# Fixed instruction lists for the first ten attention steps and the first MLP group

## The chip, the cores and the metric

One core of a Trainium2 chip runs the whole program. The metric is device time in microseconds (us), the median of several executions. One execution is also recorded by the hardware profiler, and every row below is read from that recording.

TensorE (PE; its weight loads are listed as PEld), VectorE (DVE), ScalarE (ACT), GpSimd (POOL) and SyncE (SP, which here only issues DMAs) each work off their own instruction stream in order, and wait on semaphores for one another.

## What is computed

Sliding-window attention with sinks, and then an MLP on its output:

```python
scores = q @ k.T / sqrt(64)                     # 4 batches, 8 heads, 768 tokens, 64 wide
keep   = (key < n_sink) | (0 <= query - key < window)     # n_sink 4, window 128
a      = softmax(where(keep, scores, -1e9))
x      = (a @ v) rearranged to [3072 tokens, 512]
h      = x @ w_in                               # 512 -> 2048
g      = h * erf(softplus(h))
out    = g @ w_out                              # 2048 -> 512
```

q, k and v arrive as float32. w_in and w_out arrive as float64, so every weight has to be rebuilt as float32 from the two 32-bit words of the double, by integer operations on VectorE.

## The kernel before

**Tiling.** The 3072 tokens are cut into 12 groups of 256 (three for each batch). Attention works on a group and a pair of heads at a time: a **step** s is group s // 4, pair s % 4, so there are 48. The MLP works on a group at a time, in 16 **blocks** of 128 hidden columns.

**A step** goes through these functions. `load` (L184) issues the DMAs of q, k and v: four for q and k, two for v, and two more for the sink rows of v in the first group of a batch. `prep` (L213) transposes q and k on TensorE; ScalarE copies the result to `kq` (L223). In the first group of a batch it also fills `sv` (L228 on ScalarE, L229 on VectorE). `score` (L239) makes the scores with 16 matmuls (L272). Its VectorE part is copy_predicated (L284) and one masked minimum for each of four blocks (L289); ScalarE takes exp (L293); a DMA moves a part of `kq` on for the next group. `norm` (L299) adds 1e-9 to the sum (L302), takes the reciprocal (L303) and scales four blocks (L307), all on VectorE. `ptrans` (L309) transposes the probabilities on TensorE (L317), ScalarE copies them to `pt` (L319), GpSimd cuts `uo` out of them (L323), VectorE makes the split sink part `sh` (L331, L332), which TensorE transposes (L338). `av` (L342) multiplies by v (L353, L361). `xfin` (L365) copies the result to `x` (L372, or L377 and L378).

**The weights.** They are cut into 32 pieces of 128 x 512 (16 of each matrix). `wload` (L421) fetches one piece of 512 KB, `wconv` (L430) makes float32 of it with three VectorE operations (L439, L442, L448), and `wsplit` (L457) makes a high part by a ScalarE cast (L461) and a low part by a VectorE subtract (L462). Raw pieces, float32 pieces and split pieces all take slots of one pool of 33 slots, 4 KB of each partition (`wpool`, tag `wo`). The last four pieces are converted in a work tile and copied over by ScalarE (L455).

**The MLP.** `hidden` (L524) makes one block of h, `act` (L537) the activation of two blocks at a time: six ScalarE passes (L545 to L550) and three VectorE operations (L552). `project` (L561) adds a block's share to the two output tiles. The first group uses the unsplit float32 weights (L529, L570) and needs no split pieces; later groups use the split ones (L533), and their `act` adds a cast (L557) and a GpSimd subtract (L558).

**The order of the work.** The code hands the whole program to a planner, which draws up each engine's instruction stream by simulated time: of the instructions that are ready it takes the one with the best priority. `at` (L380) sets that from a place `a` on a common scale (256 units for each block) and an offset by kind of work (L45). The first group's 16 blocks have the places 16 to 31, the second group's 32 to 47. `pos` (L385) gives a step's place, the table `plan` (L389) those of its parts. In `make_mlp` an act comes after its two blocks, a projection four blocks (`LAG`) behind its block. The conversions follow a rate (`W0`, L505), with five loads ahead (`WQ`); the splits have fixed places (L419), from 21 to 37 on that scale. Nothing but data ties the order of VectorE, TensorE and SP; only the score and av matmuls of a step are held in one order by `follow` (L204).

Of the kernel before, what the change touches and what calls it, by code (L numbers as in the profile page):

```python
# [19 lines left out]
P = 128  # L20
# [16 lines left out]
W0, W1 = 10, 7  # L37
WQ = 5

# [6 lines left out]
UB = 3  # L46
RING = 2
# [3 lines left out]
def kernel(  # L51
# [38 lines left out]
    for i, s in enumerate((n_sink, window)):  # L90
        nc.scalar.dma_start(words[:, i, :], s.bitcast(I32).partition_broadcast(P))
# [33 lines left out]

    def dcopy(dst, src):
        nc.sync.dma_start(dst, src)

    def fast_path():
        with ExitStack() as st:  # L130
# [51 lines left out]
            stp = {}  # L182

            def load(s):  # L184
                g, c = divmod(s, NPAIR)
                b, gb = divmod(g, GPB)
                d = stp[s] = {}
                for nm, src in (("q", q), ("k", k), ("v", v)):
# [3 lines left out]
                    for h in range(2):  # L192
                        nc.sync.dma_start(
# [3 lines left out]
                if gb == 0:  # L197

                    sr = d["sv"] = d["v"][: 2 * SW, 0].rearrange("p h d -> p (h d)")
                    nc.gpsimd.memset(sr, 0.0)  # L200
                    for h in range(2):
                        nc.sync.dma_start(sr[SW * h : SW * h + SW, 64 * h : 64 * h + 64], v[b, 2 * c + h, :SW, :])
# [10 lines left out]
            def prep(s):  # L213
# [4 lines left out]
                for j, t in enumerate((d["k"], d["q"])):  # L218
                    for i in range(2):
                        nc.tensor.transpose(  # L220
# [3 lines left out]
                if g % GPB == 0:  # L224
                    x = tp[:, 0, :SW].rearrange("p (o t) -> p o t", o=1)
                    nc.scalar.copy(kq[:, c, :3, P:], x.broadcast_to([P, 3, SW]))
                    for r0 in (0, 32):
                        nc.scalar.copy(sv[r0 : r0 + 32, c, :], d["sv"])  # L228
                    nc.vector.tensor_tensor(sv[64:96, c, :], d["sv"], sv[:32, c, :].bitcast(F32), op=ALU.subtract)  # L229

            def core(s):

                prev = None
                if s - AL >= NE:
                    prev = av(s - AL)
                if s < NSTEP:
                    score(s, prev)

            def score(s, prev):  # L239
# [3 lines left out]
                d = stp[s]  # L243
                d["sum"], d["neg"] = (
# [3 lines left out]
                ps, both = [], None  # L248
# [12 lines left out]
                dx = KB + 80  # L261
                X = [80, 80 + dx]
                lo, hi = slice(0, 64), slice(64, P)
                for i in range(2):
                    qt = kq[:, c, 3 + i, :]
                    kt = kq[:, c].rearrange("p n t -> p (n t)")
                    for hf, r0, n, x in ((lo, KB * i, KB + 64, X[i]), (hi, KB * i + 64, KB + 80, X[i] - 80)):
                        for h in (1, 0):
# [3 lines left out]
                                nc.tensor.matmul(ps[h][hf, x : x + n], qt[r, hf], kt[r, r0 : r0 + n], start=True, stop=True),  # L272
                            )

# [451 lines left out]
```

## Time and profile before

| | us |
|---|---|
| median of 3 executions (lowest, highest) | 765.98 (763.82, 767.38) |
| the profiled execution | 765.26 |
| its span, from the first to the last instruction | 763.3 |
| TensorE busy | 718.0 (94%) |
| VectorE busy | 526.5 (69%) |
| ScalarE busy | 535.0 (70%) |
| GpSimd busy | 202.6 (27%) |

The shares are means over the whole span, which has two very different parts: about 130 us in which the weights are fetched and rebuilt and the first group is computed, and the eleven groups after it. A share has to be read for each of the two. A matmul row's length is modelled by the profiler, and consecutive instructions of one engine overlap by about 0.1 us in the rows, so a sum of lengths is a little more than the time taken.

### The profile page before, as it was taken

Reading aid. Unit: us, or ns where it says so; the run is one execution under the profiler, and the core shown is the slowest. Engines: PE = TensorE matmul, PEld = TensorE weight load, DVE = VectorE, ACT = ScalarE, POOL = GpSimd, SP = SyncE. Lnnn points to the kernel's source line nnn. Section 1 sums busy time; section 2 is a strip of 40 time slices with the busy share of each in tenths; the row PEclk is TensorE's granted clock in tenths of the full one; section 3 lists DMA queues with packets and bytes.
Section 4 is the critical chain, followed back from the end, with each engine's and each line's share of the span. In section 5 each row is a group of like instructions: output and inputs, shape, how many; then the busy total and the mean of one; then the engine's idle time right before and its main releaser. Section 6 shows DMA issues by size and latency. Waiting matters only on the chain.

```text
span 763.3 us, 14942 instructions
## 1 busy us (share of the span) xinstructions
PE 718.0 (94%) x5168; PEld 598.2 (78%) x5168; DVE 526.5 (69%) x1509; ACT 535.0 (70%) x1261; POOL 202.6 (27%) x212
## 2 busy tenths in 40 slices
PE   2577998999999999999999999999999999999997
PEld 2345664887888898888888888888888888888885
DVE  6978998888676576576586586586576586584352
ACT  2356578897786687677787687687686687686473
POOL 1211220133322223232322232332322232322122
PEclk8679998999999999999999999999999999999999
DMA  6776530211211211211121211111111111100000
GB/s 203 218 231 198 218 86 15 76 23 26 61 44 31 67 45 25 63 31 32 56 49 30 59 42 37 55 41 29 56 38 42 56 46 36 39 12 1 28 1 32
DMA packets 100595, 47.33 MB, mean 62 GB/s; under 512 B 89248, under 2 KB 93344, under 8 KB 100512
## 3 DMA queue, kind: packets, MB, share of 16 engines
q1 hardware_dynamic: 100224, 46.29, 21.8%
q8 instruction: 43, 0.70, 0.4%
q14 instruction: 40, 0.33, 0.1%
q10 hardware_dynamic: 288, 0.00, 0.0%
HBM read 37.88 MB, written 6.29 MB: 58 GB/s over the span
## 4 chain that ended last, share of the span: by engine, by line
PE 76%; DVE 10%; ACT 6%; DMA 4%; issue 2%; SPq 1%; POOL 1%; ACTq 0%; DVEq 0%; POOLq 0%
PE o L570 30%; PE h L533 27%; PE av L361 5%; PE ps L272 4%; PE tqk L220 3%; PE tp L317 3%; PE h L529 2%; DVE pst L307 2%; DVE acc L552 1%; ACT u L550 1%; DMA ws<-in_moe_w_out_dram 1%; PE ts L338 1%; DVE w L442 1%; ACT pst L293 1%; DMA out_dram<-ot 1%
## 5 line engine op out<-in xcount | busy, mean ns | idle before, releaser
L570 PE MATMUL o<-wt,g 128*128 128x512 f32 x1056 | 270.0, 399 | 1.1 <-POOL g L558 0.5
L570 PEld LDWEIGHTS o<-wt,g 128*128 128x128 f32 x1056 | 189.0, 188 | 36.5 <-POOL g L558 1.3
L533 PE MATMUL h<-xh,wt 128*128 128x256 f32 x1408 | 203.7, 282 | 1.8 <-DVE acc L552 1.1
L533 PEld LDWEIGHTS h<-xh,wt 128*128 128x128 f32 x1408 | 184.7, 189 | 11.4 <-DVE acc L552 1.8
L558 POOL TENSOR_TENSOR g<-acc,g 128x512 fp32r<-128x512 f32 x88 | 114.7, 1303 | 291.7 <-DVE g L557 182.7
L550 ACT ACTIVATE u<-r 128x512 f32<-128x512 f32 x288 | 165.0, 623 | 13.5 <-DVE wf L448 4.4
L323 POOL TENSOR_SCALAR_AFFINE_SELECT uo<-pt 128x512 f32<-128x512 f32 (+1 forms) x96 | 83.1, 887 | 252.5 <-ACT pt L319 231.8
L552 DVE SCALAR_TENSOR_TENSOR acc<-u,acc 128x512 f32<-128x512 f32 x176 | 128.4, 730 | 19.1 <-ACT u L550 2.8
L552 DVE SCALAR_TENSOR_TENSOR acc<-u,h 128x512 f32<-128x512 f32 x88 | 60.4, 687 | 108.3 <-POOL g L558 60.3
L533 PE MATMUL h<-xl,wt 128*128 128x256 f32 x704 | 111.2, 279 | 0.0
L293 ACT ACTIVATE pst<-pst,kq 128x144 f32<-128x144 f32 x192 | 77.4, 405 | 25.7 <-DVE kq L289 24.6
L533 PEld LDWEIGHTS h<-xl,wt 128*128 128x128 f32 x704 | 94.2, 188 | 0.0
L545 ACT ACTIVATE r<-h 128x512 f32<-128x512 f32 x96 | 57.0, 593 | 25.8 <-PE h L533 24.9
L546 ACT ACTIVATE r<-r 128x512 f32<-128x512 f32 x96 | 61.1, 637 | 2.0
L547 ACT ACTIVATE r<-r 128x512 f32<-128x512 f32 x96 | 60.6, 631 | 2.6
L307 DVE TENSOR_SCALAR pst<-pst,kq 128x144 f32<-128x144 f32 x192 | 57.2, 360 | 1.5
L317 PE MATMUL tp<-ident,pst 128*128 128x128 f32 x192 | 36.4, 291 | 17.5 <-DVE pst L307 17.2
L557 DVE CAST g<-acc 128x512 fp32r<-128x512 f32 x88 | 44.3, 504 | 12.1 <-PE o L570 8.1
L223 ACT COPY kq<-tqk 128x512 f32<-128x512 f32 x48 | 28.0, 585 | 33.7 <-PE tqk L220 31.6
L361 PE MATMUL av<-uo,v 128*64 128x128 f32 (+1 forms) x512 | 50.1, 328 | 1.2 <-POOL uo L323 1.2
L377 ACT CAST xh<-av 128x256 fp32r<-128x256 f32 x44 | 16.0, 365 | 49.2 <-PE av L361 49.2
L272 PE MATMUL ps<-kq 64*64 64x208 f32 (+1 forms) x768 | 49.5, 369 | 0.0
(78 smaller groups left out, 723.0 us busy)
## 6 DMA issues: line engine op xcount, KB each, us to landing
ws<-in_moe_w_in_dram SPq DMA_DIRECT2D x16, 512.0 KB, 5.8
ws<-in_moe_w_out_dram SPq DMA_DIRECT2D x16, 512.0 KB, 5.0
q<-in_q_dram SPq DMA_DIRECT2D x96, 64.0 KB, 2.2
k<-in_k_dram SPq DMA_DIRECT2D x96, 64.0 KB, 2.2
v<-in_v_dram SPq DMA_DIRECT2D x64, 96.0 KB, 2.4
out_dram<-ot SPq DMA_DIRECT2D x24, 256.0 KB, 2.0
v<-in_v_dram SPq DMA_DIRECT2D x32, 64.0 KB, 2.2
kq<-kq SPq DMA_DIRECT2D x32, 64.0 KB, 2.0
```

Of the source, the lines that this page charges most:

```text
L272: nc.tensor.matmul(ps[h][hf, x : x + n], qt[r, hf], kt[r, r0 : r0 + n], start=True, stop=True),
L293: nc.scalar.activation(y, y, AF.Exp, bias=d["neg"][:, i, h : h + 1], scale=-1.0, accum_out=d["sum"][:, i, h : h + 1])
L307: nc.vector.tensor_scalar_mul(p, p, sm[:, i, h : h + 1])
L323: nc.gpsimd.affine_select(out=uo[:, :, i1:, e, :], in_=pt[:, :, i1:, :], pattern=[[0, 2], [0, 2 - i1], [-sg, P]], compare_op=op, fill=0.0, ...
L361: prev, nc.tensor.matmul(o, x[:, h, :], y[:, h, :], start=False, stop=(m == len(ops) - 1), skip_group_check=True)
L533: nc.tensor.matmul(o, wt[NC * j + c][:, p, fs], xt[e][:, c, :], start=(m == 0), stop=(m == len(ops) - 1))
L546: nc.scalar.activation(r, r, AF.Square, bias=b_v, scale=-0.5)
L547: nc.scalar.activation(r, r, AF.Square, bias=b_r)
L550: nc.scalar.activation(u, r, AF.Square, bias=b_a[i], scale=CS)
L552: nc.vector.scalar_tensor_tensor(out=acc, in0=u, scalar=CC[i] * CS**2, in1=x, op0=ALU.add, op1=ALU.mult)
L558: nc.gpsimd.tensor_tensor(gl, acc, gh.bitcast(F32), op=ALU.subtract)
L570: nc.tensor.matmul(self.acc[g, i], gt[e][:, n0 : n0 + P], w, start=(f == 0 and m == 0), stop=(f == NF - 1 and m == len(ops) - 1),)
```

## The change

Three lists name the work of the first ten steps and the first group's 16 blocks, one each for SP (`LOADS`), VectorE (`VEC`) and TensorE (`TEN`). In them q and v load a step's q and k, and its v; L loads, C converts a weight piece, D finishes all conversions under way; p, s, t, u and a are prep, score, the two transposes of ptrans and av on TensorE; f, n, w, k, x are the score's VectorE part, norm, `sh`, `sv` and xfin; H, A and P are hidden, act and project. A class `Line` ties each instruction of an engine to the one before it, so the order of the lists is the engine's order. On TensorE that holds to the end of the lists, on SP to place 20, on VectorE to place 50 (`CEND`), which is two blocks into the third group.

Conversions are cut into their three operations, and `fill` puts one operation of each conversion under way between the dependent operations of norm and act. A converted piece is written at once to half of a slot that two pieces share, for all 32. The splits have new places: 26 (cast) and 27.5 (subtract) for the first four, 30 and 31.5 for the next five, then on to 45 and 46.5. Steps 2 and 3 keep their probabilities in pool slots of their own, and the first steps' transposes use other PSUM tiles. Four things change engine: half of the q and k loads of steps 0 and 1 (SP to ScalarE), the two `sv` copies of steps 0 to 3 (ScalarE to GpSimd), and the scaling in norm of steps 4 to 7 (VectorE to ScalarE). Later steps' places move by fractions of a block.

```diff
+CEND = 50.0
 WQ = 5
+HI = 6.0
+LO = 4.5
+LOADS = (
+    "q0 q1 L0 v0 q2 v1 L1 q3 v2 L2 q4 v3 L3 L4 q5 v4 L5 v5 L6 L7 q6 v6 L8 L9 L10 L11 q7 v7 L12 L13 L14 L15 L16 L17 q8 v8 "
+    "L18 L19 L20 L21 L22 q9 v9 L23 L24 L25 L26 L27 L28 L29 L30 L31"
+)
+VEC = (
+    "f0 C0 D f1 n0 w0 n1 w1 k0 f2 k1 C1 D n2 w2 k2 f3 C2 D n3 w3 k3 f4 C3 n4 D f5 w4 C4 C5 n5 D C6 C7 D w5 C8 C9 A1 C10 C11 "
+    "D f6 x4 C12 A3 n6 C13 D w6 C14 C15 A5 C16 C17 D f7 x5 C18 C20 A7 n7 C19 C21 D w7 C22 C23 A9 C24 C25 D f8 x6 C26 A11 n8 "
+    "C27 D w8 C28 C29 A13 x7 C30 C31 D f9 A15"
+)
+TEN = (
+    "p0 s0 p1 s1 p2 t0 u0 s2 t1 u1 p3 a0 x0 s3 a1 x1 t2 u2 p4 s4 a2 x2 t3 u3 p5 s5 a3 x3 t4 u4 H0 H1 H2 H3 p6 t5 u5 a4 s6 "
+    "H4 H5 P0 P1 H6 P2 t6 u6 H7 P3 p7 a5 s7 H8 H9 P4 P5 H10 P6 t7 u7 p8 H11 P7 a6 s8 H12 H13 P8 a7 P9 t8 H14 P10 u8 p9 H15 "
+    "P11 s9"
+)
@@ load @@
-                        nc.sync.dma_start(
+                        (nc.scalar if s < 2 and h and nm != "v" else syn).dma_start(
@@ the lists' order @@
+            class Line:
...
+                    def run(*a, **k):
+                        ins = f(*a, **k)
+                        if self.on:
+                            self.last = follow(self.last, ins)
+                        return ins
...
+            vec, ten, syn = (Line(x) for x in (nc.vector, nc.tensor, nc.sync))
@@ prep, now prep and sinks @@
-                        nc.scalar.copy(sv[r0 : r0 + 32, c, :], d["sv"])
+                        (nc.gpsimd.tensor_copy if s < NE else nc.scalar.copy)(sv[r0 : r0 + 32, c, :], d["sv"])
@@ score @@
+                if s in (2, 3):
+                    t = wpool.tile([P, 2 * DM], F32, tag="wo", name=f"pst_{s}")
...
-                    if s == 1:
+                    if s in (1, 2):
                         ps.append(ps_h.tile([P, 2, GT], F32, tag="h", name=nm).rearrange("p a t -> p (a t)"))
-                    elif s == 2:
-                        ps.append(ps_o.tile([P, DM], F32, tag="o", name=nm))
@@ norm @@
-                nc.vector.tensor_scalar_add(sm, sm, 1.0e-9)
-                nc.vector.reciprocal(sm, sm)
+                vec.tensor_scalar_add(sm, sm, 1.0e-9)
+                fill()
+                vec.reciprocal(sm, sm)
+                fill()
...
+                        if 4 <= s < 8:
+                            nc.scalar.activation(p, p, AF.Copy, scale=sm[:, i, h : h + 1])
+                        else:
+                            vec.tensor_scalar_mul(p, p, sm[:, i, h : h + 1])
@@ ptrans and strans @@
-                tp = ps_t.tile([P, 2, 2, P], F32, tag="t", name=f"tp_{s}")
+                pool, tag = (ps_o, "o") if s < 6 else (ps_t, "t")
+                tp = pool.tile([P, 2, 2, P], F32, tag=tag, name=f"tp_{s}")
@@ wconv @@
+                if wn // 2 not in pair:
+                    pair[wn // 2] = wpool.tile([P, 2, DM], F32, tag="wo", name=f"wf_{wn // 2}")
+                t = wf[n] = pair[wn // 2][:, wn % 2, :]
...
+                vec.tensor_scalar(ti, w[:, :, 1], 0x07FFFFFF, 3, op0=ALU.bitwise_and, op1=ALU.logical_shift_left)
+                yield
+                vec.scalar_tensor_tensor(
+                    out=ti, in0=w[:, :, 1], scalar=-0x40000000, in1=ti, op0=ALU.bitwise_and, op1=ALU.bitwise_or
+                )
+                yield
+                vec.scalar_tensor_tensor(
+                    out=ti, in0=w[:, :, 0], scalar=29, in1=ti, op0=ALU.logical_shift_right, op1=ALU.bitwise_or
+                )
-                wf[n] = wpool.tile([P, 2 * DM], F32, tag="wo", name=f"wf_{n}")[:, :DM]
-                nc.scalar.copy(wf[n], t)
+            def fill():
+                for w in list(todo):
+                    try:
+                        next(w)
+                    except StopIteration:
+                        todo.remove(w)
@@ the places, and the loop over all work @@
+            for n in order:
+                add(LEAD + NF + use(n) - HI, "h", n)
+                add(LEAD + NF + use(n) - LO, "l", n)
+            for a, _, nm, j in sorted(ev):
+                vec.on, ten.on, syn.on = a < CEND, a <= last, a < LEAD + 4
+                what, fn = acts[nm]
+                with at(a, what):
+                    fn(j)
@@ act @@
-                nc.vector.scalar_tensor_tensor(out=acc, in0=u, scalar=CC[i] * CS**2, in1=x, op0=ALU.add, op1=ALU.mult)
+                self.vec.scalar_tensor_tensor(out=acc, in0=u, scalar=CC[i] * CS**2, in1=x, op0=ALU.add, op1=ALU.mult)
+                self.fill()
```

## Rows read from the trace of the kernel before

**Rows 1.** The page's 40 slices of the span: busy tenths of TensorE and VectorE.

```profile
PE   2577998999999999999999999999999999999997
DVE  6978998888676576576586586586576586584352
```

**Rows 2.** Windows: span, each engine's busy us (instructions), TensorE clock, DMA share, GB/s.

```profile
10.00:20.00 10.00, 1.59 (x18) 0.87 (x11) 7.29 (x25) 2.59 (x11) 0.00 (x0) 0.76 1.00 339
8.70:129.90 121.20, 91.78 (x490) 60.11 (x483) 108.94 (x317) 69.58 (x183) 21.51 (x19) 0.85 0.57 178
129.90:146.30 16.40, 16.40 (x126) 11.37 (x125) 11.34 (x32) 12.13 (x30) 1.68 (x2) 0.96 0.13 29
146.30:203.90 57.60, 56.64 (x421) 49.15 (x421) 46.33 (x125) 46.99 (x116) 16.25 (x17) 1.00 0.17 42
319.00:376.95 57.95, 57.86 (x445) 49.68 (x444) 38.07 (x115) 43.11 (x107) 17.97 (x19) 1.00 0.17 42
```

**Rows 3.** Waits of TensorE and VectorE, 8.7 to 129.9: total us, times, longest.

```profile
PE tp L317 <- DVE pst L307: 15.6, 3, 10.5
PE h L529 <- DVE gf L552: 4.6, 3, 3.6
...
DVE kq L302 <- ACT pst L293: 3.4, 2, 2.3
```

**Rows 4.** Groups by form, VectorE, 8.7 to 129.9: xcount | busy, mean ns | idle.

```profile
L442 DVE SCALAR_TENSOR_TENSOR w<-ws,w 128x512 int32<-128x512 int32 x32 | 22.2, 700 | 0.0
L448 DVE SCALAR_TENSOR_TENSOR wf<-ws,w 128x512 int32<-128x512 int32 x28 | 19.6, 702 | 0.1
L439 DVE TENSOR_SCALAR w<-ws 128x512 int32<-128x512 int32 x32 | 13.9, 436 | 2.3 <-DMA ws<-in_moe_w_in_dram 2.1 <-DMA ws<-in_moe_w_out_dram 0.2
...
L462 DVE TENSOR_TENSOR wt<-wf,wt 128x512 fp32r<-128x512 f32 x14 | 10.0, 722 | 0.5 <-ACT wt L461 0.5
```

**Rows 5.** Timeline of VectorE: start, length, instructions [idle before <-releaser].

```profile
8.39 0.32 DVE L160 TENSOR_SCALAR mask<-mask 128x144 bf16<-128x144 bf16 x2
...
40.29 1.28 DVE L442 SCALAR_TENSOR_TENSOR w<-ws,w 128x512 int32<-128x512 int32 x2
...
48.37 0.90 DVE L284 COPY_PREDICATED ps<-tri,ps 64x256 f32<-64x256 int8 x2
...
51.38 0.17 DVE L302 TENSOR_SCALAR kq<-kq 128x4 f32<-128x4 f32 x1 [1.08 <-ACT pst L293]
...
51.80 0.91 DVE L307 TENSOR_SCALAR pst<-pst,kq 128x144 f32<-128x144 f32 x4
...
53.04 0.23 DVE L332 TENSOR_TENSOR sh<-pst,sh 128x64 fp32r<-128x64 f32 x1
...
129.64 0.69 DVE L552 SCALAR_TENSOR_TENSOR gf<-u,gf 128x512 f32<-128x512 f32 x1
```

**Rows 6.** Timeline of TensorE and ScalarE, same columns.

```profile
8.33 3.27 PE L272 MATMUL ps<-kq 64*64 64x208 f32 x32
...
84.72 3.62 PE L529 MATMUL h<-xf,wf 128*128 128x256 f32 x16
...
7.58 0.58 ACT L223 COPY kq<-tqk 128x512 f32<-128x512 f32 x1 [4.54 <-PE tqk L220]
```

**Rows 7.** Timeline of GpSimd: the cuts of steps 1, 2 and 7.

```profile
33.12 3.46 POOL L323 TENSOR_SCALAR_AFFINE_SELECT uo<-pt 128x256 f32<-128x256 f32 x2 [2.06 <-ACT pt L319]
46.47 1.09 POOL L323 TENSOR_SCALAR_AFFINE_SELECT uo<-pt 128x256 f32<-128x256 f32 x2 [9.90 <-ACT pt L319]
...
108.24 5.20 POOL L323 TENSOR_SCALAR_AFFINE_SELECT uo<-pt 128x512 f32<-128x512 f32 x2 [14.25 <-ACT pt L319]
```

**Rows 8.** Page: the exp group on ScalarE (columns as Rows 4).

```profile
L293 ACT ACTIVATE pst<-pst,kq 128x144 f32<-128x144 f32 x192 | 77.4, 405 | 25.7 <-DVE kq L289 24.6
```

**Rows 9.** DMA issues: loads of weight pieces, count, size, us to landing.

```profile
ws<-in_moe_w_in_dram SPq DMA_DIRECT2D x16, 512.0 KB, 5.8
```

**Rows 10.** Timeline of SP: the first stores of results.

```profile
146.26 0.90 SPq L496 DMA_DIRECT2D out_dram<-ot  x2
```

More of the change, by code (lines that the diff above doesn't have):

```diff
@@ L258, in score @@
                         ps.append(both[:, h, :])
-                dx = KB + 80
-                X = [80, 80 + dx]
-                lo, hi = slice(0, 64), slice(64, P)
+                d["ps"] = ps, both
                 for i in range(2):
@@ new lines, in fast_path, with add, hid, act @@
+            mlp = make_mlp(work, ps_h, ps_o, vec, ten, fill)
+            gs, hp, ev = {}, {}, []
+            def add(a, nm, j):
+                ev.append((a, len(ev), nm, j))
+            def hid(m):
+                g, f = divmod(m, NF)
+                if f % 2 == 0:
+                    hp[m // 2] = mlp.hid_tile(m)
+                mlp.hidden(hp[m // 2], xp[g], f)
+            def act(m):
+                gs[m // 2] = mlp.act(hp.pop(m // 2), m, m < NF)
+            def proj(w):
+                g, f = divmod(w, NF)
+                mlp.project(gs[w // 2], g, f)
@@ new lines, in res, with use @@
+            def res(k):
+                g, i = divmod(k, 2)
+                nc.sync.dma_start(out[k * P : (k + 1) * P, :], mlp.result(g, i))
+            def use(n):
+                return NC * (n // NC) if n < 16 else n - 16 + LAG
+            order = sorted(range(32), key=use)
+            acts = {
+                "q": ("load", loadqk), "v": ("load", loadv), "p": ("prep", prep), "k": ("prep", sinks), "s": ("core", score),
+                "f": ("core", soft), "n": ("norm", norm), "t": ("ptrans", ptrans), "w": ("ptrans", sinkw), "u": ("ptrans", strans),
+                "a": ("av", av), "x": ("xfin", xfin), "H": ("hid", hid), "A": ("act", act), "P": ("proj", proj), "R": ("res", res),
+                "L": ("wl", lambda j: wload(order[j])), "C": ("wc", lambda j: todo.append(wconv(order[j], j))), "D": ("wc", drain),
+                "h": ("ws", whigh), "l": ("ws", wlow),
+            }
@@ new lines, in fast_path @@
+            lines = [words(x) for x in (LOADS, VEC, TEN)]
+            known = {w for x in lines for w in x}
+            done, a = set(), LEAD - 10
+            while any(lines):
+                before = len(done)
+                for x in lines:
+                    while x and all(w in done for w in needs(*x[0]) if w in known):
+                        w = x.pop(0)
+                        a = LEAD + w[1] if w[0] == "H" else a + 0.012
+                        add(a, *w)
+                        done.add((w[0], len(done)) if w[0] == "D" else w)
+                assert len(done) > before, [x[:1] for x in lines]
@@ new lines, in fast_path @@
+            last = a
+            for s in range(NE, NSTEP + AL):
+                a = pos(s)
+                for nm, z, n in (
+                    ("a", a + 0.139, s - AL), ("x", a + 1.11, s - AL), ("n", a + 1.12, s), ("p", a - 2.87, s), ("k", a - 2.869, s),
+                    ("s", a + 0.14, s), ("f", a + 0.141, s), ("t", a + 2.15, s), ("w", a + 2.151, s), ("u", a + 2.152, s),
+                    ("q", a - 3.84, s), ("v", a - 3.839, s),
+                ):
+                    if NE <= n < NSTEP and (nm, n) not in done and (nm != "k" or n // NPAIR % GPB == 0):
+                        add(max(z, last + 0.01) if nm in "ntwu" else z, nm, n)
@@ new lines, in fast_path @@
+            for m in range(NG * NF):
+                g, f = divmod(m, NF)
+                a = m + LEAD
+                for nm, z in (("H", 0.4 if f == 0 else 0.0), ("P", LAG + 0.3), ("A", 0.5)):
+                    if (nm != "A" or f % 2 == 1) and (nm, m) not in done:
+                        add(a + z, nm, m)
+                if f == NF - 1:
+                    for i in range(2):
+                        add(a + LAG + 0.31, "R", g * 2 + i)
+            for n in order:
+                add(LEAD + NF + use(n) - HI, "h", n)
+                add(LEAD + NF + use(n) - LO, "l", n)
@@ L528, in hidden @@
                 for c in range(NC):
[L529 removed]
+                    self.ten.matmul(o, wf[NC * j + c][:, fs], xt[0][:, c, :], start=(c == 0), stop=(c == NC - 1))
                 return
```

242 lines of the change are left out of this document (103 added, 139 removed).

## The prediction

> **What bounds the kernel now.** I read the 40 slices first, for where TensorE is short of work [rows 1]. From the eighth slice on, about 130 us in, it is at nine tenths or more; in the first seven it is not, and there VectorE is the one that stays near full. So the later groups are bounded by TensorE, which the change gives nothing there, and the head is the place to look. The windows give the size: from 8.7 to 129.9 us VectorE is busy 108.94 of 121.20, TensorE 91.78, and part of that at a granted clock of 0.85 in the mean, that is partly at 1.2 GHz; from 319 to 376.95, one whole group of the steady part, TensorE is busy 57.86 of 57.95 and VectorE 38.07 [rows 2]. The waits say who holds whom in the head: TensorE's longest are for VectorE, 15.6 us for the scaled probabilities of three steps and 4.6 for the activation [rows 3]. VectorE itself waits little, and its largest piece of work is the weights: 32 of each of three operations [rows 4].
>
> So the head is a sum on VectorE. Its end I take at the last activation of the first group, at 129.64 + 0.69 = 130.3 [rows 5]. From there TensorE works without a gap (16.40 of 16.40) to the first group's store at 146.26 [rows 2, 10]. If VectorE reaches that activation earlier, all that follows moves with it.
>
> **The change part by part.** Prices first. *A conversion*: the two later operations have 0.70 us, the first 0.436, and neighbours overlap by about 0.1 (two take 1.28), so 0.60 + 0.60 + 0.34 = 1.54 when other work lies between, and 1.83 by the rows' full lengths when it runs alone [rows 4, 5]. *A softmax part f*: from 48.37 to the start of the idle time before 51.38, that is 50.30: 1.92. *norm and w*: from 51.38 to 53.27: 1.9, of which the four scalings 0.82 to 0.91 [rows 5].
>
> *What VectorE's list holds up to A15, against the same stretch before.* All 32 conversions, f0 to f8, n0 to n8, w0 to w8 and the eight activations lie in both. Different are:
> - Splits: 14 subtracts lie before 129.9 now [rows 4]; with the new places four are left there (the next five have place 31.5, behind A15). Ten fewer at 0.62 (between 0.60 and 0.722): -6.2.
> - Scaling of steps 4 to 7 goes to ScalarE: four times 0.82: -3.3. ScalarE pays 16 passes; no row shows a scaled copy, the nearest is exp of the same shape at 0.405 with its bias and sum [rows 8], so between nothing and 6.5 us in all. ScalarE is busy 69.58 of 121.20, so I take it as hidden; its cover is the list's D or f between n and w, 1.9 us or more against four passes of 1.6. Without that cover w, and so u, wait for the difference.
> - f9 comes into the list: +1.9. x7: +0.4.
> - Six conversions (0, 1, 2, 3, 13, 27) run with no second one between their operations: six times 0.29 = +1.7 (from nothing to 32 times 0.29 = 9.3 if pairs did not overlap either).
>
> 108.94 - 6.2 - 3.3 + 1.9 + 0.4 + 1.7 = 103.4 us of work.
>
> *Idle time of VectorE.* Now 121.20 - 108.94 = 12.3. I walked the three lists with these prices, the masks being ready at 8.7 [rows 5]. In the list's order VectorE's work ends near these times: f0 10.6, f1 14.4, w1 18.0, f2 20.7, f3 26.9, f4 33, w4 38.5, w5 46, A1 51, A3 60, A5 68, A7 78, A9 87, A11 96, A13 107, A15 115. The waits left in it: n4 stands right behind f4, and n5 nearly behind f5; the last exp comes 1.08 after f, as before 51.38 [rows 5], so 1.1 + 0.7. f2 and f4 wait for their scores, 0.5 + 0.9, since s2 stands behind u0 and s4 behind a1 on TensorE. A1 waits 0.9 for H1. Together 4.1; the bounds are 0 and today's 12.3. I take 4.1, as each of the larger waits of today (weights that have not landed, 2.1; sums not ready, 3.4 [rows 3, 4]) has other work put in its place.
>
> So A15 ends at 8.7 + 103.4 + 4.1 = 116.2, against 130.3: **14.1 us earlier**.
>
> *SP.* Everything in its list queues behind its waits: v3 waits for a0, v4 for a1, v5 for a2, v6 for a3, v7 for a4, q for the prep two steps back, and the pieces L and the copies of `kq` queue behind them. The tightest are L8 (behind v6, a3 at about 38, landed 5.8 later [rows 9], near 44) for C8 at 46, and L12, L13 (behind v7, a4 at about 47, landed 54) for C12 at 57. The cover is 2 to 3 us; if a3 is later than 40, VectorE waits for all that is above it. Volume is no limit: 32 pieces of 512 KB and ten steps of some 0.4 MB are 21 MB, at 339 GB/s [rows 2] 62 us of the 107. Half the first q and k loads go to ScalarE's queue: four issues before its first copy, which waits 4.54 us for TensorE anyway [rows 6]; that may bring p0 about 1 us forward (0 to 1.5), but the masks at 8.7 hold f0, so nothing.
>
> *TensorE.* Its work before A15 is that of the same stretch now, 91.78 us, some of it at 1.2 GHz [rows 2]; that fits the 107 us of VectorE's list. Two blocks of hidden take 3.6 us at 2.4 GHz, two steps' scores 3.27 in the first steps [rows 6]; with these in the walk every score, hidden block and projection is there when VectorE's list calls for it, the nearest being s7 for f7 and s8 for f8, about 2 us ahead. Holding pst of steps 2 and 3 in other slots and the transposes in other PSUM tiles takes waits away and adds no instruction: nothing, since the list's own order already decides. The same goes for the shared slots; the four ScalarE copies that fall away are as well hidden as the scaling that comes in.
>
> *GpSimd.* It takes over eight copies of `sv`. None is in the trace; its cuts of `uo` are the nearest. Two of 128x256 took 1.09 us at 46.47 and 3.46 at 33.12; step 7's two took 5.20 [rows 7]. In the walk I used 3.46 for steps 0 to 3, which the transposes and scores around a0 to a3 nearly cover. The Trainium skill (SBUF — State Buffer, Who interferes with whom) says that a VectorE instruction with two SBUF inputs contends with a GpSimd instruction that reads SBUF. That speaks against a list that packs such instructions closely; the rows at 33.12 and 108.24 agree with it, and what it would do is the first rival.
>
> *The second group.* The ten splits left out, and those that were late anyway, make 28 for it. Its VectorE work becomes 38.07 + 28 x 0.62 = 55.4 of 57.6 us; before it held 46.33 with 11 splits and took 57.60 [rows 2], about what later groups take. The cost lies between nothing (four blocks lie between a block and its projection) and the 19.9 us that VectorE idles in a steady group, all on the path. I take 2, near the lower end, as 11 splits cost nothing that can be seen.
>
> *Sum.* Span 763.3 - 14.1 + 2.0 = 751.2. The profiled execution is 765.26, 1.96 over its span: 753.2. It was 0.7 below the median of 765.98: **754.0**.
>
> **Rivals.** *GpSimd is held.* Each cut takes 5.2 instead of 3.46, and the copies stretch with it. s3 stands behind a0, s4 behind a1, t2 behind a1, H0 behind a3, so delays add up over four steps: 4 x 1.7 = 7 us, some of it covered: 754 + 6 = 760. For it: the row at 108.24. Against: when f waits, VectorE rests, and GpSimd runs free (1.09).
>
> *VectorE's fixed order holds ready work* (the slower side). Now the planner fills waits with whatever is ready; from the change on an instruction that waits for an exp, a score or an activation holds conversions and splits behind it, in the head and, by CEND, in the whole second group. If the head keeps all its 12.3 us of idle time, and the second group the 19.9 it has now with 28 splits on top (38.07 + 17.4 + 19.9 = 75.4, that is 17.8 beyond 57.6), the change is -14.1 + 8.2 + 17.8 = +12: 778. It turns slower than the 0.5% once idle time in the head and loss in the second group pass 22 of these 30 us. For it: steady VectorE idles a third although TensorE is full, so some of its waits are real. Against: those waits come of VectorE being ahead; with 97% to do it lags and they vanish. Half of it gives 763 to 768.
>
> *The lists change nothing*: the planner's order was already as good, or waits simply move. 766. For it: VectorE is busy 90% of the head now. Against: 10 splits and 16 scalings do leave it.
>
> **How the numbers follow.** The forecast of 754 has 0.67, GpSimd held 0.13 (760), half of the held order 0.08 (766), all of it 0.07 (778), nothing 0.05 (766). The low end is no idle time (-4.1), no loss in the second group (-2.0) and overlapped conversions (-1.7): 746. The high end is today's 12.3 us of idle time: 754 + 8.2 = 762, and 763 to take in the second rival's near part. Within 0.5%, about what a measurement of this kernel can tell from no change, is 762.2 to 769.8. So faster 0.80, same 0.13, slower 0.07.
>
> **What would show it.** VectorE over 95% busy from 8.7 on; the first blocks of hidden on TensorE at about 40 us; A15's last operation at about 116 instead of 130.3; the first store at about 132 instead of 146.3; the second group's store 57 to 60 us after it; the later stores at today's spacing. VectorE waiting for DMA at C8 or C12 would show SP's cover gone, cuts of `uo` over 4 us in steps 0 to 3 the first rival, a second group over 65 us the slower one. I am wrong altogether if the first store moves by less than 4 us, or if it moves and the groups after it are longer.

## The result, and the profile after

| us | before | after |
|---|---|---|
| median (lowest to highest), 4 runs each | 766.16 (763.82 to 767.38) | 753.52 (752.94 to 753.62) |
| the profiled execution | 765.26 | 753.57 |
| its span | 763.3 | 751.8 |

The ratio is 0.9837, with a 95% interval of 0.9813 to 0.9861: the changed kernel is 12.6 us faster. The forecast was 754.0.

The total came out as forecast, but it is made of other terms. The head gained more than forecast, and the second group gave back more. The page's 40 slices of the changed kernel, as in [rows 1]:

```profile
PE   4798999898999999999999999999999999999996
DVE  7899998988676577576576576676676576664352
```

TensorE is now at eight tenths or more from the third slice on; before, it was at seven in the third and fourth and fell to eight again in the seventh. The windows give the sizes (columns as in [rows 2]). The changed kernel's come first, then those of the kernel before; each set is cut near its own kernel's first two stores:

```profile
8.70:54.54 45.84, 38.18 (x258) 26.41 (x251) 39.96 (x146) 28.85 (x93) 11.17 (x22) 0.89 0.72 203
54.54:120.40 65.86, 60.32 (x302) 38.88 (x301) 64.45 (x157) 46.89 (x111) 4.64 (x6) 1.00 0.55 186
8.70:120.40 111.70, 98.50 (x558) 65.28 (x551) 104.41 (x302) 75.74 (x204) 15.81 (x28) 0.95 0.62 193
...
0.00:128.20 128.20, 107.84 (x608) 71.89 (x609) 116.97 (x349) 85.03 (x221) 18.85 (x43) 0.96 0.58 178
128.20:200.00 71.80, 65.06 (x488) 52.77 (x487) 59.62 (x159) 53.11 (x132) 21.03 (x23) 1.00 0.16 40
200.00:751.80 551.80, 545.17 (x4075) 471.44 (x4075) 351.35 (x986) 398.22 (x914) 145.78 (x155) 1.00 0.15 39
```

```profile
0.00:146.30 146.30, 110.43 (x623) 73.36 (x624) 125.50 (x376) 83.95 (x215) 26.06 (x36) 0.87 0.51 156
146.30:203.90 57.60, 56.64 (x421) 49.15 (x421) 46.33 (x125) 46.99 (x116) 16.25 (x17) 1.00 0.17 42
203.90:763.30 559.40, 550.98 (x4129) 475.65 (x4127) 354.65 (x1009) 404.01 (x933) 160.34 (x159) 1.00 0.15 40
```

TensorE's busy time over the whole span is the same, 718.1 us, so the 11.5 us between the spans are idle time of TensorE. Stretch by stretch that idle time was 35.9, 1.0 and 8.4 us and is now 20.4, 6.7 and 6.6: the head gains 15.5, the second group loses 5.8, and the rest gains 1.8.

By these bounds the head is 18.1 us shorter, 128.2 against 146.3. Its TensorE busy time fell as well, by 2.6, at a mean granted clock of 0.96 instead of 0.87: less of it ran at 1.2 GHz. Those 2.6 come back as busy time behind 128.2. To compare equal work, I counted every matmul at the median time of its form in the trace of before (from its start to the next one's) and compared the moments at which both kernels have done the same sum. The changed kernel leads by 14.2 us at 34 us of such work, by 18.2 at 88, by 12.0 at 112, by 8.7 at 148, and then by 9 to 12 to the end; another way of taking a form's time moves most of these by less than 1 us. So about 9 us are lost while the second group is computed.

The timelines show the ends of the head. First VectorE, then TensorE, then SP's stores (columns as in [rows 5]; lines left out between them):

```profile
9.83 0.90 DVE L234 COPY_PREDICATED ps<-tri,ps 64x256 f32<-64x256 int8 x2 [1.13 <-PE ps L234]
...
36.56 0.17 DVE L234 TENSOR_SCALAR kq<-kq 128x4 f32<-128x4 f32 x1 [1.35 <-ACT pst L340]
...
53.86 0.68 DVE L234 SCALAR_TENSOR_TENSOR gf<-u,gf 128x512 f32<-128x512 f32 x1
...
118.93 1.49 DVE L234 SCALAR_TENSOR_TENSOR gf<-u,gf 128x512 f32<-128x512 f32 x2
```

```profile
41.99 7.53 PE L234 MATMUL h<-xf,wf 128*128 128x256 f32 x32
...
110.61 1.51 PE L234 MATMUL h<-xh,wt 128*128 128x256 f32 x8
...
120.43 1.07 PE L234 MATMUL h<-xh,wt 128*128 128x256 f32 x8
...
121.79 2.73 PE L234 MATMUL o<-wf,gf 128*128 128x512 f32 x6
...
124.47 1.02 PE L234 MATMUL o<-wf,gf 128*128 128x512 f32 x2
```

```profile
127.31 1.60 SPq L531 DMA_DIRECT2D out_dram<-ot  x2
199.15 0.85 SPq L531 DMA_DIRECT2D out_dram<-ot  x2
257.03 0.84 SPq L531 DMA_DIRECT2D out_dram<-ot  x2
```

All instructions that go through `Line` are recorded with its line, L234, so they are told apart by their tiles: `gf` is the activation of the first group, `xh` and `wt` are the split operands that only later groups use. A15, the first group's last activation, ends at 118.93 + 1.49 = 120.42, and the first store is issued at 127.31 instead of 146.26 [rows 10], 18.95 earlier. The next store follows 71.8 us later, the one after it 57.9 later, about as far apart as in the steady part before.

### The profile page after: what moved, and what is told of

Same layout as the page of the kernel before. It is cut to its first block, busy times and chain, and to the rows that moved or that the text cites. A ratio compares the mean times of both kernels' runs of the same rounds, so it can differ in the third digit from the quotient of the medians.

```text
span 751.8 us, 14883 instructions
## 1 busy us (share of the span) xinstructions
PE 718.1 (96%) x5168; PEld 596.1 (79%) x5168; DVE 527.9 (70%) x1493; ACT 536.4 (71%) x1265; POOL 185.7 (25%) x220
## 4 chain that ended last, share of the span: by engine, by line
PE 74%; DVE 17%; ACT 4%; issue 1%; DMA 1%; SPq 1%; ACTq 0%; DVEq 0%
PE h L234 29%; PE o L234 29%; DVE wf L234 6%; PE av L234 6%; PE ps L234 4%; PE tqk L234 3%; DVE wt L234 2%; DVE pst L234 2%; ACT pst L340 2%; PE tp L234 2%; DVE gf L234 2%; DVE ps L234 1%; PE ts L234 1%; DVE acc L234 1%; DMA v<-in_v_dram 1%
## 5 line engine op out<-in xcount | busy, mean ns | idle before, releaser
L234 PE MATMUL o<-wt,g 128*128 128x512 f32 x1056 | 272.1, 399 | 1.2 <-POOL g L656 0.8
L234 PEld LDWEIGHTS o<-wt,g 128*128 128x128 f32 x1056 | 189.9, 188 | 38.0 <-POOL g L656 1.6
L234 PE MATMUL h<-xh,wt 128*128 128x256 f32 x1408 | 204.8, 283 | 2.4 <-DVE acc L234 2.4
L656 POOL TENSOR_TENSOR g<-acc,g 128x512 fp32r<-128x512 f32 x88 | 116.2, 1320 | 365.5 <-DVE g L234 316.5
L234 PEld LDWEIGHTS h<-xh,wt 128*128 128x128 f32 x1408 | 183.7, 188 | 13.4 <-DVE acc L234 3.4
L234 DVE SCALAR_TENSOR_TENSOR acc<-u,acc 128x512 f32<-128x512 f32 x176 | 126.8, 720 | 21.6 <-ACT u L647 7.9
L234 DVE SCALAR_TENSOR_TENSOR acc<-u,h 128x512 f32<-128x512 f32 x88 | 60.3, 685 | 82.6 <-POOL g L656 51.4
L234 PE MATMUL h<-xl,wt 128*128 128x256 f32 x704 | 110.9, 279 | 0.0
L375 POOL TENSOR_SCALAR_AFFINE_SELECT uo<-pt 128x512 f32<-128x512 f32 (+1 forms) x96 | 62.9, 678 | 155.7 <-ACT pt L371 155.6
L234 PEld LDWEIGHTS h<-xl,wt 128*128 128x128 f32 x704 | 94.1, 188 | 0.3 <-DVE wf L234 0.2
L234 PE MATMUL ps<-kq 64*64 64x208 f32 (+1 forms) x768 | 50.5, 374 | 6.1 <-ACT kq L262 4.6
L234 DVE TENSOR_SCALAR pst<-pst,kq 128x144 f32<-128x144 f32 x176 | 52.6, 359 | 1.5
L234 DVE CAST g<-acc 128x512 fp32r<-128x512 f32 x88 | 38.9, 442 | 17.4 <-PE o L234 12.2
L234 PE MATMUL av<-uo,v 128*64 128x128 f32 (+1 forms) x512 | 49.8, 327 | 0.0
L234 DVE CUSTOM_DVE_ANT_0 pst<-ps,mask 128x144 f32<-128x144 f32 x192 | 47.6, 304 | 1.6
L234 DVE COPY_PREDICATED ps<-tri,ps 64x256 f32<-64x256 int8 (+1 forms) x100 | 41.6, 419 | 7.2 <-PE ps L234 3.2
```

The costliest lines, as they stand in the source:

```text
L234: ins = f(*a, **k)
L375: nc.gpsimd.affine_select(out=uo[:, :, i1:, e, :], in_=pt[:, :, i1:, :], pattern=[[0, 2], [0, 2 - i1], [-sg, P]], compare_op=op, fill=0.0, ...
L656: nc.gpsimd.tensor_tensor(gl, acc, gh.bitcast(F32), op=ALU.subtract)
```

## Experiments

The forecast had three open points: which part of the change earns the gain in the head, why the second group pays, and whether what I took to be free was free. Times stand against 753.5 for the changed kernel; the kernel before had medians of 765.4 to 765.9 beside these runs.

### Which part earns the gain

**VectorE's order set free.** TensorE and SP keep their lists.

```diff
-CEND = 50.0
+CEND = -99.0
```

> Against the changed kernel (753.5): VectorE's instructions are not tied to one another, all else as it is, so the planner draws up VectorE's order. Prediction's reading (the list takes 8 us of waits out of the head): A15 ends 5 to 8 us later, 758 to 762. Rival (the gain is the work that left the head, and any order does): 752 to 755.

Measured: 789.5 us, 1.0313 of before (1.0289 to 1.0338), 36 us above the changed kernel. The waits of TensorE between 8.7 and 140 us (total, times, longest), and the longest one in its timeline:

```profile
PE ts L234 <- DVE sh L234: 13.9, 3, 13.1
...
PE o L234 <- DVE gf L234: 8.5, 2, 7.5
```

```profile
95.42 0.66 PE L234 MATMUL ts<-ident,sh 128*128 128x128 f32 x2 [13.10 <-DVE sh L234]
```

This misses both expected ranges by far. The planner's own order on VectorE calls for `sh` late, while TensorE's list has that transpose in a fixed place, and everything behind it on TensorE stands still for 13.1 us. Here a held order of one engine became a cost because the engine that feeds it went by another order.

**TensorE's and SP's order set free.** VectorE keeps its list.

```diff
-                vec.on, ten.on, syn.on = a < CEND, a <= last, a < LEAD + 4
+                vec.on, ten.on, syn.on = a < CEND, False, False
```

> Against the changed kernel (753.5): TensorE and SP are not tied to their lists, VectorE stays tied. Prediction's reading (the head is VectorE's sum and TensorE follows): 752 to 757. Rival (the three lists only work together, as VectorE's order without the others loses what it won): over 765.

Measured: 766.9 us (1.0016 of before, 1.0004 to 1.0028): the whole gain is gone, as the rival said. The longest waits between 8.7 and 140 us, of VectorE and of TensorE behind it:

```profile
DVE wf L234 <- DMA ws<-in_moe_w_in_dram: 14.8, 1, 14.8
...
PE ps L234 <- DVE kq L234: 11.4, 1, 11.4
```

SP's timeline gives the reason for this wait: the first weight piece that it issues, in this kernel and then in the changed one.

```profile
22.40 2.73 SPq L234 DMA_DIRECT2D ws<-in_moe_w_in_dram  x5
```

```profile
3.51 0.34 SPq L234 DMA_DIRECT2D ws<-in_moe_w_in_dram  x1
```

When its order is free, SP first issues the loads of q, k and v for several steps, and the first piece only at 22.40. VectorE's list has that piece near its front, and VectorE stands 14.8 us before it; TensorE's next score stands behind VectorE. In the changed kernel VectorE has no wait for a DMA from 8.7 to 120.4. The wait points at SP's list; what TensorE's list is worth by itself is not shown, as the two were not freed one at a time.

**Scaling back on VectorE** in steps 4 to 7.

```diff
-                        if 4 <= s < 8:
+                        if False:
```

> Against the changed kernel (753.5): the scaling in norm of steps 4 to 7 goes back to VectorE. Prediction's term: A15 ends 3.3 us later, 756 to 757.5. Rival (VectorE has room for it in the waits behind n4 and n5): 753 to 754.5.

Measured: 757.3 us (0.989 of before, 0.9872 to 0.9909), 3.75 more. The last activation of the first group on VectorE, to be read beside the same row at 118.93 above:

```profile
121.96 1.49 DVE L234 SCALAR_TENSOR_TENSOR gf<-u,gf 128x512 f32<-128x512 f32 x2
```

The head ends 3.0 later, near the 3.3 of that term.

**The splits moved forward again**, by four places, in the changed kernel.

```diff
-HI = 6.0
-LO = 4.5
+HI = 10.0
+LO = 8.5
```

> Against the changed kernel (753.5): all splits four places earlier (first at 22, last at 41), about where they stood before. Some 10 low parts return to the head's VectorE work (+6.2 us on A15's end) and leave the second group. Theory (VectorE's sum bounds both): the head loses about 6, the second group gains about 6, 752 to 756. Rival (late splits are what costs, the head has room): 747 to 750. Rival (the move of the splits is the whole gain): 759 to 761.

Measured: 753.4 us (0.983 of before, 0.9796 to 0.9865), no change in the time, though the head is longer. Its last activation, and the windows' row for the second stretch:

```profile
124.13 1.49 DVE L234 SCALAR_TENSOR_TENSOR gf<-u,gf 128x512 f32<-128x512 f32 x2
```

```profile
128.20:200.00 71.80, 67.84 (x509) 55.72 (x507) 57.05 (x155) 54.17 (x136) 21.39 (x23) 1.00 0.16 40
```

Twelve low parts now lie before A15 instead of four. A15 ends at 125.62, 5.2 later, and TensorE is busy 2.8 us longer between 128.2 and 200 (67.84 against 65.06). These eight low parts cost as much on one side of A15 as on the other.

**The splits moved back in the kernel before**, and nothing else of the change.

```diff
-                split.setdefault(n // 4 * 4 + n % 4 + 5 if n < 16 else n - 16 + LAG + 2, []).append(n)
+                split.setdefault(NF - 5 + (4 * (n // 4) if n < 16 else n - 16 + LAG), []).append(n)
```

> The kernel before with one edit: its splits have about the changed kernel's places (27 for the first four, to 46). Prediction's sum: ten low parts leave the head, A15 -6, the second group gives 1 to 6 back: 760 to 765 against 765.4. Rival (late splits cost as much as they bring): 765 to 768. Rival (the move of the splits is most of the change): 754 to 757.

Measured: 764.9 us, 0.9991 of before (0.9976 to 1.0006): no change that can be told, at the border of the first two expected ranges. The last activation of the first group on VectorE, to be read beside 129.64 in [rows 5]:

```profile
127.08 0.68 DVE L552 SCALAR_TENSOR_TENSOR gf<-u,gf 128x512 f32<-128x512 f32 x1
```

With five low parts before A15 instead of 14, A15 ends only 2.6 us earlier, not 6. By the count of TensorE's work this execution led by 4.9 us at 82 us of work and by less than 0.2 at 92. It is the longest of the ten, 769.7 us, so its later part says little. Moving the splits out of the head thus brought no gain for the whole that can be seen, in the new order or in the old.

**PSUM tiles and probabilities as before** for the first steps (the second edit stands twice, once for each of ptrans's transposes).

```diff
-                if s in (2, 3):
+                if False:
...
-                pool, tag = (ps_o, "o") if s < 6 else (ps_t, "t")
+                pool, tag = ps_t, "t"
```

> Against the changed kernel (753.5): steps 2 and 3 keep their probabilities in the ring of two again, and the transposes of the first six steps use the PSUM tiles that prep and av use too. Prediction: nothing, since the lists' own order decides, 752.5 to 754.5. Rival (with the lists fixed, a slot not yet free stops an engine, and all behind it): 757 or more.

Measured: 755.2 us in the median of three executions (0.9865 of before, 0.9845 to 0.9885); a fourth took 2467.5 for an unknown reason and is left out. That is 1.6 more, though the two intervals overlap. A15 ends at 122.03, 1.6 later as well:

```profile
120.54 1.49 DVE L234 SCALAR_TENSOR_TENSOR gf<-u,gf 128x512 f32<-128x512 f32 x2
```

This is the edit that I had put at nothing. It takes back two things, and the run does not part them.

### Why the second group pays

**The late low parts not computed on VectorE.** 28 of the 32 low parts of the weights are filled by a DMA with the unsplit weights. This kernel leaves the subtractions out, so it does not compute the same function.

```diff
-                vec.tensor_tensor(d[:, 1, :], wf.pop(n), d[:, 0, :].bitcast(F32), op=ALU.subtract)
+                if order.index(n) < 4:
+                    vec.tensor_tensor(d[:, 1, :], wf.pop(n), d[:, 0, :].bitcast(F32), op=ALU.subtract)
+                else:
+                    nc.sync.dma_start(d[:, 1, :].bitcast(F32), wf.pop(n))
```

> Leaves part of the work out: the low parts of the 28 later pieces are not subtracted but filled by a DMA from the float32 piece, so VectorE loses 28 x 0.62 = 17.4 us of the second group, and SP issues 28 DMAs of 256 KB. Against the changed kernel (753.5). Theory (the late splits on VectorE are what the second group gives back): the 9 us it gives back at equal TensorE work fall to 0 to 2, 744 to 747. Rival (the attention steps' chain through the fixed order is slow by itself, with or without splits): at most 3 us, 750 to 753.

Measured: 747.4 us (0.9763 of before, 0.9742 to 0.9783), 6.1 less. First the windows' row of this kernel, then TensorE's waits in the changed kernel from 128.2 to 200, then those of this kernel from 120 to 200:

```profile
128.20:200.00 71.80, 70.95 (x543) 59.48 (x544) 48.11 (x146) 57.48 (x141) 20.65 (x26) 0.98 0.21 56
```

```profile
PE h L234 <- DVE acc L234: 2.1, 4, 0.7
PE ts L234 <- DVE sh L234: 2.0, 4, 0.6
PE tp L234 <- DVE pst L234: 1.7, 2, 1.5
PE o L234 <- POOL g L656: 0.8, 2, 0.4
```

```profile
PE av L234 <- ACT pt L371: 2.1, 1, 2.1
PE tp L234 <- DVE pst L234: 0.5, 1, 0.5
PE ts L234 <- DVE sh L234: 0.3, 1, 0.3
```

TensorE's 6.7 us of idle time in that stretch are many short waits, nearly all for VectorE; without the subtractions 0.85 us of idle time is left. So about 6 of the 9 us that are given back are the late low parts on VectorE. VectorE is not full there (59.62 of 71.80); it also waits, 5.7 us of it for ScalarE's exps. My reading is that what becomes due meanwhile stands behind the subtractions. That is argued and not shown: the two runs below that move the subtractions within the group changed nothing.

**Half of the late low parts on GpSimd** (14 pieces).

```diff
-                vec.tensor_tensor(d[:, 1, :], wf.pop(n), d[:, 0, :].bitcast(F32), op=ALU.subtract)
+                (nc.gpsimd if order.index(n) % 2 and order.index(n) > 4 else vec).tensor_tensor(d[:, 1, :], wf.pop(n), d[:, 0, :].bitcast(F32), op=ALU.subtract)
```

> Against the changed kernel (753.5): 14 of the 28 low parts that fall into the second group are subtracted by GpSimd instead of VectorE, same places. VectorE loses 14 x 0.62 = 8.7 us there. Theory (what the second group gives back, about 9 us at equal TensorE work, is VectorE's sum of work): most of it comes back, 747 to 749, and TensorE is busy over 69 of the 71.8 us from 128.2 on. Rival (the fixed order holds ready work behind waits): the sum matters little, 752 to 754. Second rival (GpSimd, slower for the same subtract and contending with VectorE, delays the g of each activation): 754 to 758.

Measured: 762.2 us (0.995 of before, 0.9933 to 0.9967), 8.6 more and beyond all three expected ranges. The profile's view of the tile `wt` on GpSimd (shortest, median and longest in ns), then waits between 120 and 200 us, then the windows' row:

```profile
L502 POOL TENSOR_TENSOR wt<-wf,wt x14: 1265/1554/4006, 98.2 to 184.1; 128x512 fp32r<-128x512 f32 x14
```

```profile
POOL wt L502 <- ACT wt L497: 14.6, 4, 7.9
DVE kq L234 <- ACT pst L340: 11.4, 4, 4.2
```

```profile
128.20:200.00 71.80, 62.46 (x441) 51.19 (x439) 53.99 (x127) 50.10 (x120) 28.52 (x26) 0.95 0.13 33
```

VectorE's work did fall (53.99 instead of 59.62), and TensorE got less done (62.46 instead of 65.06). The subtractions wait on GpSimd for ScalarE's casts, 7.9 us at the longest, and whatever is next on GpSimd, cuts of `uo` and subtractions of `g`, stands behind them. The price had moved into another in-order queue. About half of it arises earlier, though: A15 ends at 124.94, 4.5 later, with the planner starting seven of GpSimd's subtractions ahead of it. The first three of these, and a VectorE operation beside them:

```profile
98.15 4.79 POOL L502 TENSOR_TENSOR wt<-wf,wt 128x512 fp32r<-128x512 f32 x3 [9.92 <-DVE gf L234]
...
98.36 1.77 DVE L234 SCALAR_TENSOR_TENSOR gf<-u,gf 128x512 f32<-128x512 f32 x1
```

The same operation of the changed kernel, at 98.21, took 0.69. So this run does not say what the second group would gain if VectorE were relieved without harm elsewhere.

**The late splits spread out**, one for each block instead of four at a time.

```diff
-                add(LEAD + NF + use(n) - HI, "h", n)
-                add(LEAD + NF + use(n) - LO, "l", n)
+                e = 3.0 - n % NC if 4 <= n < 16 else 0.0
+                add(LEAD + NF + use(n) - HI - e, "h", n)
+                add(LEAD + NF + use(n) - LO - e, "l", n)
```

> Against the changed kernel (753.5): the places of the splits of w_in pieces 4 to 15 are spread, one a block, where four of them share one place now (five low parts stand in a row on VectorE, 4.1 to 4.6 us); none is later than now. Theory (sum of work): 752.5 to 754, as the sum stays. Rival (the rows of five hold sh and activation behind them): the bursts go and 3 to 5 us come back, 748.5 to 751.

Measured: 753.7 us (0.9837 of before, 0.9802 to 0.9871): no change. So it is not the cause that up to five low parts stand in a row on VectorE.

**The same splits one place earlier**, ahead of the step's other work (those used from the sixth block on).

```diff
-                add(LEAD + NF + use(n) - HI, "h", n)
-                add(LEAD + NF + use(n) - LO, "l", n)
+                e = 1.0 if use(n) >= 5 else 0.0
+                add(LEAD + NF + use(n) - HI - e, "h", n)
+                add(LEAD + NF + use(n) - LO - e, "l", n)
```

> Against the changed kernel (753.5): all splits but the first four are one place earlier, so that the rows of five low parts stand between f and n of a step (where VectorE waits for exp) instead of between n and sh. Same work, five low parts return to the head. Theory of waits (in the fixed order VectorE's work and its waits for exp add up, 5.7 us of waits): 3 to 5 us come back, 748.5 to 750.5. Theory of the sum alone: 752.5 to 754.

Measured: 753.3 us (0.9843 of before, 0.9821 to 0.9864): no change either. VectorE's waits for the exps between 120 and 200 us, in the changed kernel and then in this one:

```profile
DVE kq L234 <- ACT pst L340: 5.7, 5, 2.3
```

```profile
DVE kq L234 <- ACT pst L340: 6.6, 4, 3.5
```

The 3 to 5 us that were to come back if the subtractions filled these waits did not; the waits stayed. Where exactly the low parts stand in the second group matters less than that they are there.

**VectorE's order free from the second group on.**

```diff
-CEND = 50.0
+CEND = 32.0
```

> Against the changed kernel (753.5): VectorE's fixed order ends at place 32, with the first group's lists, so the planner orders the second group again. Theory (sum of work): within 1.5 us, 752 to 755. Rival (the fixed order holds ready work): the second group's loss goes as far as the planner can fill waits, 746 to 750.

Measured: 758.0 us (0.9899 of before, 0.9862 to 0.9935), 4.5 more. Its last activation of the first group:

```profile
128.82 0.68 DVE L234 SCALAR_TENSOR_TENSOR gf<-u,gf 128x512 f32<-128x512 f32 x1
```

The planner, left to itself, takes the splits early: 21 of the 32 low parts end before A15 instead of four, the last one starts at 141.3, and A15 ends 9.1 later. The time is only 4.5 longer, so behind A15 this kernel loses less than the changed one. The fixed order is thus what keeps the splits out of the head. Whether it costs the second group something by itself the run does not show, as it moves the splits as well.

### A version beyond

**Scaling on ScalarE in steps 4 to 13**, so in the second group too.

```diff
-                        if 4 <= s < 8:
+                        if 4 <= s < 14:
```

> Against the changed kernel (753.5): the scaling in norm goes to ScalarE for steps 8 to 13 as well, 6 x 0.82 = 4.9 us less for VectorE in the second group, next to 28 low parts; ScalarE is busy 53.1 of 71.8 us there. Theory (VectorE's work and its waits add up there; leaving out the low parts brought 6.1 us for 17.4): 1.5 to 4 us come back, 749.5 to 752. Rival (the chain from exp to the transposes only grows by ScalarE's queue): 753 to 757.

Measured: 751.8 us (0.982 of before, 0.9792 to 0.9847), 1.7 below the changed kernel's median, though the two intervals overlap. The second stretch by the windows:

```profile
128.20:200.00 71.80, 66.44 (x504) 56.27 (x503) 54.43 (x128) 57.77 (x145) 22.77 (x24) 0.98 0.16 41
```

VectorE has 5.2 us less to do than in the changed kernel, and TensorE does 1.4 more. That goes the expected way, but the time alone does not show a gain.

## Why the prediction was right, point by point

The time was right, and so was what bounds the head. That the total came out within 1 us is luck: several terms behind it were wrong and cancelled.

**What bounds the head: right.** VectorE's list sets its end. Added VectorE work moved A15 nearly one to one (the scaling by 3.0 us for 3.3, eight low parts by 5.2 for 5.0).

**The sum on VectorE: right.** 103.4 was forecast from 8.7 on, 104.41 measured. The small terms (f9, x7, conversions that run alone) were not measured one by one.

**The gain of the ten splits (−6.2): right for A15, wrong for the total.** The sum booked them as a gain, with 2 us for the second group against it. Moving eight of them forward in the new kernel, or nine back in the old one, changed nothing in the total that can be seen. The gain needs the common order: without VectorE's list the kernel was slower than before, without the other two it was as slow as before. How much the order earns was not measured. Taking back the scaling costs 3.75 us and the slots and PSUM tiles about 1.6; if the parts add up, that leaves about 7 of the 12.6 for the order and for what no run took back (the `sv` copies on GpSimd, the first loads on ScalarE's queue, the shared weight slots, the conversions cut in three).

**Scaling to ScalarE (−3.3, hidden): right**, 3.0 at A15 and 3.75 in the time. The 16 scaled copies took 405 ns each in the mean, 5.3 us in all. The price was thus near the upper bound of 6.5, and the cover held: VectorE did not wait for them, and of TensorE only weight loads did, for 1.8 us in all.

**VectorE's idle time (4.1): too small.** It is 7.3, and the windows say where: 5.9 of it up to 54.54, the end of A1, and 1.4 in the 65.86 us behind. The first f waited 1.13 for its score although the masks were ready (I had it start at once), n4 waited 1.35 and n5 0.98 for the last exp (1.1 and 0.7 forecast). So VectorE was busy 87% up to A1 and 98% from there on, 93% over all and not over 95%. The walk's milestones came 3.5 us late at A1 (54.5 for 51) and stayed near that to A9 (90.8 for 87); A15 ended at 120.4 for 116.2, so 9.9 earlier than before and not 14.1.

**SP: right.** No wait of VectorE for a DMA in the head. The run with SP and TensorE free shows the wait that the list avoids, 14.8 us.

**Slots and PSUM tiles (nothing): wrong by about 1.6 us,** as far as one run whose interval overlaps can tell. I had reasoned that the list's order already decides; it decides only where a tile is free when the list calls for it.

**GpSimd: right.** The first rival needed cuts above 4 us. In steps 0 to 3 they took 1.02 to 1.47 for two, and two copies of `sv` 0.63 to 0.69:

```profile
20.13 1.02 POOL L375 TENSOR_SCALAR_AFFINE_SELECT uo<-pt 128x256 f32<-128x256 f32 x2
...
37.06 1.47 POOL L375 TENSOR_SCALAR_AFFINE_SELECT uo<-pt 128x256 f32<-128x256 f32 x2 [8.25 <-ACT pt L371]
```

The 3.46 at 33.12 and the 5.20 at 108.24 [rows 7] were not the price of a full VectorE as such; what ran beside a cut mattered. The pair at 20.13 fell beside VectorE operations that read PSUM, and its second cut took 0.64. The second cut at 37.06 fell beside two conversion operations and took 1.09, and the first of the two at 108.24 took 4.61 with seven operations of two SBUF inputs beside it.

**TensorE after A15 (16 us as now): wrong, too long by 9.** I had added today's 16.4 us to A15. Before, TensorE was behind by that much work when VectorE came to its end. Now only about 7 us are left (120.42 to 127.31): of the first group TensorE had just eight projection matmuls to do (`o<-wf,gf`, 121.79 to 125.49), and it had already taken up blocks of the second group, from 110.61 on. So the store came 4.7 us ahead of the forecast (127.3 for 132), though A15 was 4.2 late.

**The second group (+2): wrong, too small by 7.5.** I priced 28 splits by the fact that 11 had cost nothing that could be seen. That was a stretch in which VectorE had 20% to spare (46.33 of 57.60 [rows 2]). The rival's mechanism, late work of VectorE with ready work behind it, is my reading of what happened here, though not shown; its own mark, a second group over 65 us from store to store, is passed with 71.8 (partly since the first store came early). But it took about 9 of its 17.8 us. About 6 of the 9 are the low parts, by the run that leaves them out. Whether the fixed order has a share in them is open: freeing it also moved the splits, and two other places for them changed nothing. Whatever else lies in it (VectorE waited 5.7 us for exps and ScalarE 5.4 for v in that stretch) was not separated.

**The sum.** Forecast: A15 −14.1, nothing behind it, second group +2, so −12.1 in the span. Measured: A15 −9.9, TensorE behind it −8.3 (together the lead of 18.2 at 88 us of work), the second group +9.5 (the lead falls to 8.7 at 148), and −2.8 later, so −11.5. Three errors, 4.2, −8.3 and 7.5, with −2.8 that I had not looked for, left 0.6 between them: the total was hit by luck, with terms that were not. The two large ones may belong together: TensorE started on the second group early and so left the head sooner, and then met VectorE's deferred work; no run parts them.

**The other rivals.** "The lists change nothing" falls with the total; its ground, that the planner was already as good, falls with the run of 789.5 only in part, since there two engines held lists. The sign "wrong altogether" came in part: the first store moved, and one group after it got longer, the second (71.8 us for 57.7 from store to store); the next was 57.9. So by its own sign the prediction failed there, and what failed is the price of the second group.

## What to carry to other kernels

Taking work out of a stretch is a gain only if the stretch that receives it has that much idle time at the moments when it is due; price it by what waits behind it there, and test it by moving it back. Treat an order fixed by hand on several engines as one thing: a part of it alone can be worse than none, as here without VectorE's list. When the bounding engine's list gets shorter, don't add today's tail behind it; ask what the other engine will have finished by then.

## What the runs showed of the hardware

**Two engines at the same subtraction.** In the changed kernel a low part's subtraction of 128x512 float32 took VectorE 0.67 to 0.69 us mostly, but up to 1.78, and in the stretch from 128.2 to 200 their mean rose to 0.84 (0.68 in the head). All 22 with no GpSimd instruction beside them took 0.675 to 0.687; the five that took over 1 us all ran beside a subtraction of GpSimd. Timelines of VectorE and GpSimd in the changed kernel:

```profile
156.03 2.82 DVE L234 TENSOR_TENSOR wt<-wf,wt 128x512 fp32r<-128x512 f32 x2
```

```profile
156.58 1.72 POOL L656 TENSOR_TENSOR g<-acc,g 128x512 fp32r<-128x512 f32 x1
```

Two that ran beside GpSimd's took 2.82 instead of about 1.3, and GpSimd's took 1.72 where its mean is 1.30 in a steady group. With 22 subtractions in that stretch at 0.84 instead of 0.68 that is an estimate of 3.5 us of VectorE, which may be part of what the second group lost; no run takes it out alone. The Trainium skill (SBUF — State Buffer, Who interferes with whom) says that a VectorE instruction with two SBUF inputs contends with a GpSimd instruction that reads SBUF, and the trace agrees. I had looked for this in the head, in the cuts of `uo`, where it was small; it came where the moved subtractions met GpSimd's own.

**GpSimd's subtraction of the same shape** took 1.27 to 4.01 us, 1.55 in the median, in the run that moved 14 low parts there, so it was no cheap place for work that VectorE does in 0.68.
